# A second layer norm that reads the raw row sums, and a new order of a planned transformer block on one core

## The chip, the core and the metric

The kernel runs on one core of a Trainium2 chip. Its engines work side by side, each through its own list of instructions in order: TensorE (PE) multiplies matrices, VectorE (DVE) and ScalarE (ACT) do element-wise work, GpSimd (POOL) and SyncE (SP) here mostly issue transfers (DMA). They wait for each other through semaphores. PE writes its results into PSUM, eight banks of 128 x 512 float32; everything else lies in SBUF, 128 partitions wide. The metric is the device time of one execution in microseconds (us), as the median of several runs.

## The reference

A pre-norm block on `x` of shape (1, 2048, 512) in bfloat16: local dilated attention, then a gated feed-forward part, each behind a layer norm and with a residual addition.

```python
def _layernorm(x, axis=-1, eps=1e-5):
    m = jnp.mean(x, axis=axis, keepdims=True)
    v = jnp.var(x, axis=axis, keepdims=True)
    return (x - m) / jnp.sqrt(v + eps)

# attention: 32 heads of 16, each row attends to itself and 7 earlier rows, 2 apart
logits = einsum("bhsd,bhswd->bhsw", q, kg) * 16 ** -0.5     # masked where the row is before 0
o = einsum("bhsw,bhswd->bhsd", softmax(logits), vg) @ wo

# feed-forward, F = 1376
gate = einsum("bsd,df->bsf", x, W_gate); up = einsum("bsd,df->bsf", x, W_up)
y = einsum("bsf,fd->bsd", where(gate > 0, gate, 0) * up, W_down)

h  = x + attention(_layernorm(x))
h2 = h + feed_forward(_layernorm(h))
```

## The kernel before

**Tiling.** The 2048 rows go in four chunks of 512 rows (`tk` 0 to 3), each made of four blocks of 128 rows (`j`). For every chunk the kernel normalizes the rows, transposes them, computes Q, K and V in transposed form (`qkv`, twelve groups of four matmuls, line 587), multiplies Q with eight shifted K on DVE (`pr`, lines 638 and 653), sums over each head on PE (`sc`, lines 644 and 689), takes exponentials on ACT (`ex`), adds and inverts the denominators (`es`, `den`, `dl`, `dr`), scales the weights (`am`, line 747), spreads them over the partitions of each head by broadcast transfers on SP (`bd`, line 763, four for each half of the window), multiplies with eight shifted V (`mu`, lines 795 and 810), and sums the eight products (`tree`): the first halving by an accumulating transfer issued by POOL (`ta`, line 838), the others on DVE (lines 798 and 832). The output projection (`wo`, line 876) follows, one group for each block of rows.

**The second norm.** `rs` (line 887) adds the projection to `x` in place and writes the row's sum to `sm`. `hnm` (line 452) multiplies this sum by -1/512 and stores the negative mean. Two steps read that: `hsq` on ACT (line 458) squares the centred row and accumulates the squares, and `hxn` on DVE (line 512) writes the centred row in bfloat16. The centred row is not divided by the standard deviation. Since the feed-forward part is a product of two linear terms, the missing factor is the reciprocal variance, and it is multiplied in at the end: `hrl` and `hre` (lines 479 and 486) form it from the accumulated squares by a logarithm and an exponential, and `o` (lines 1006 and 1008) scales the down projection with it and adds the residual. Centred rows are transposed either on PE (`htp`, line 546, with a copy from PSUM, `hte`, line 562) or by a transposing transfer on SP (`htd`, line 535), which is the way of chunks 1 to 3.

**The feed-forward part.** The gate and up matmuls (`mm0` to `mm4`, line 949) take the transposed rows; ACT copies the up part (`ue`, line 953) and applies the rectifier to the gate part (`ge`, line 956), DVE multiplies them (`gu`, line 977). The last 96 of the 1376 columns are computed with rows on the partitions (`mm5`, line 916; `ge5`, `gu5`, lines 922 and 926) and transposed on SP (`gtd`, line 935). The down projection (`dn`, line 1000) reads eleven such tiles, the first eight in one step and the last three in another. In the last chunk the last block of rows is cut into columns 0 to 256, 256 to 384 and 384 to 512 (`dn3`, `dn4`, `dn5`). Results are stored by SP (`os`, line 1014), that of `dn5` by the ACT queue; those of chunks 0 and 1 go through an accumulating transfer (`oa`, line 1029) and a store (line 1032).

**Setup and head.** The first loads stand in a fixed order in `setup()`: row blocks of `x` on SP and ACT, three of the four chunks of the Q and K weights on the ACT queue (line 324) and the fourth on SP (line 339), behind a small POOL memset (line 338) that delays it. In chunk 0 the first six groups of Q and K are cut into pieces: `a` and `d` (row blocks 0 and 1, first two weight chunks), `b` (both blocks, last two weight chunks), `c` and `e` (row blocks 2 and 3). One `a` or `d` piece is two matmuls of 128 columns.

**What sets the order.** The work is not emitted where it is written. `add` collects 760 steps, each with its engine, an assumed duration and what it waits for, and gives it the number at its place in the list `RANK` as its priority. `order` then takes the steps strictly by rank. On each engine the steps therefore run in the order of their ranks, whatever the assumed durations are. The durations, the due times of loads (`XT`, `WT`) and the model of transfers (`dq`) decide only which of several equal buffers a step gets: the one that by the plan comes free first.

Of the kernel before, what the change touches and what calls it, by code (L numbers as in the profile page):

```python
# [93 lines left out]
class Plan:  # L94
# [21 lines left out]
    def order(self):  # L116
# [4 lines left out]
        while left:  # L121
# [80 lines left out]
def kernel(  # L202
# [23 lines left out]
    PRE = ((3,0),(3,1))  # L226
    PRD = ()
# [8 lines left out]
    CS = 512  # L236
# [21 lines left out]
    eps_t = sb.tile([P, 1], F32, name="eps_t")  # L258
# [57 lines left out]
    def setup():  # L316
# [11 lines left out]
        nc.gpsimd.memset(eps_t[:], EPS)  # L328
# [49 lines left out]
    XT = (3.1, 3.25, 4.1, 5.9, 7.15, 8.65, 9.0, 9.4, 12.9, 14.85)  # L378
    WT = (8.35, 8.35, 7.0, 11.5, 16.15, 25.5, 19.6, 29.0)
# [16 lines left out]
    TTM, DTG, ATE = 0.0845, 0.35, 0.3  # L396
# [5 lines left out]
    MM, TP = 0.2165, 0.057  # L402
    SW = 0.21
    PEL = 0.22
    A5, A10, AX, AS = 0.485, 0.91, 0.75, 0.21
    AL = 0.13
    D2, D5, D10, D20, D40, DST, DSM = 0.33, 0.61, 0.60, 1.14, 2.2, 0.61, 0.09
# [29 lines left out]
    def layernorm(tk, src, dst_slots, pr, groups, on_act, residual=None):  # L437
# [7 lines left out]
        for grp in groups:  # L445
            ag, nms = [], {}
            gk = str(grp[0]) if len(groups) > 1 else ""
            lo, hi = grp[0], grp[-1] + 1
            for j in grp:
                if residual:  # L450
                    def f_nm(j=j):
                        V.tensor_scalar(out=mv.t[:, j, 0:1], in0=sm.t[:, j:j + 1], scalar1=-1.0 / D,  # L452
                                        scalar2=None, op0=ALU.mult)

                    h = src[j][1] if tk in RPE else None

                    def f_sq(j=j, h=h):
                        nc.scalar.activation(out=junk[:, j % 2, :], in_=h.t[:] if h else x_sm[:, tk * BPC + j, :],  # L458
                                             func=ACT.Square,
                                             bias=mv.t[:, j, 0:1], scale=1.0, accum_out=sq.t[:, j:j + 1])  # L460

                    a = nms[j] = add((ln + "nm" + gk, tk), "DVE", DSM, f_nm, [src[j][0]], pr, take=[mv], use=[sm], lat=DL)
                    ag.append(add((ln + "sq" + gk, tk), "ACT", 0.66 if h else 0.72, f_sq, [a], pr,
                                  take=[sq], use=[mv] + ([h] if h else []), lat=AL))
# [625 lines left out]
```

## Time and profile before

| what | value |
|---|---|
| median of three timed runs | 192.83 us (192.31 to 192.97) |
| the profiled execution, its own time | 193.22 us |
| its span, first to last instruction | 191.3 us |
| granted PE clock, mean | 0.997 of full speed |
| busy: PE, DVE, ACT, POOL | 185.3, 149.6, 115.2, 18.5 us |
| moved by DMA | 26.44 MB |

The profile comes from one execution. Busy times are sums of instruction durations on one engine, overlaps counted once; ends of matmuls are modelled, so a busy PE need not be at its peak. PEld is the loading of stationary weights, which overlaps with PE's matmuls. A line such as L512 is line 512 of the kernel. "x16 | 5.1, 348" after a group means sixteen instructions, 5.1 us busy in all, 348 ns each on the mean. A q behind an engine's name (SPq, ACTq) means its sequencer, which issues transfers and waits.

### The profile page before, as it was taken

To read this page: it belongs to the slowest core of one execution; us is meant where nothing else is said; L and a number is where in the kernel's file an instruction comes from. 1 tells how busy PE (TensorE), PEld (TensorE's weight loads), DVE (VectorE), ACT (ScalarE), POOL (GpSimd) and SP (SyncE) were. 2 spreads that over 40 slices of the span, in tenths; PEclk is the share of its full clock that TensorE was granted. 3 is DMA by queue.
4 is the path that set the end of the run, shared out by engine and by line. 5 is a ranking of instruction groups with operands and counts; after the bars stand their busy time and mean duration, and the time that the engine had idled before them with its cause. 6 is when DMAs were issued, how large, how long until landed. Compare 5 with 4: busy or idle time off the path is not lost.

```text
span 191.3 us, 3033 instructions
## 1 busy us (share of the span) xinstructions
PE 185.3 (97%) x1101; PEld 96.5 (50%) x1120; DVE 149.6 (78%) x246; ACT 115.2 (60%) x236; POOL 18.5 (10%) x34
## 2 busy tenths in 40 slices
PE   7899999999999999999999999999999999999993
PEld 7795555544455444644445544444446444445452
DVE  6899999999999999999999987999627503212632
ACT  2589999976748967753454875144855528517500
POOL 3000002500000042000055000042100000000000
PEclk9999999999999999999999999999999999999998
DMA  5998464992068589993479916779900460120302
GB/s 159 331 351 327 102 157 84 200 196 45 0 258 228 168 154 193 183 279 61 88 131 186 203 33 139 164 151 186 211 4 0 82 165 0 31 82 0 82 25 88
DMA packets 26718, 26.44 MB, mean 138 GB/s; under 512 B 12528, under 2 KB 22608, under 8 KB 26704
## 3 DMA queue, kind: packets, MB, share of 16 engines
q1 hardware_dynamic: 23248, 16.39, 30.9%
q0 software_dynamic: 2736, 8.91, 25.1%
q10 hardware_dynamic: 720, 0.95, 1.5%
q8 instruction: 9, 0.15, 0.3%
q14 instruction: 5, 0.04, 0.1%
HBM read 8.42 MB, written 2.10 MB: 55 GB/s over the span
## 4 chain that ended last, share of the span: by engine, by line
PE 94%; DMA 3%; issue 1%; ACTq 0%; DVE 0%
PE bank L949 36%; PE bank L587 22%; PE bank L1000 20%; PE bank L876 7%; DMA wqk_sb<-in_A_wqkv_dram 3%; PE bank L644 3%; PE bank L916 3%; PE bank L546 2%; PE bank L689 1%; PE bank L720 0%; ACTq L324 0%; ACTq L322 0%; DVE row L1008 0%
## 5 line engine op out<-in xcount | busy, mean ns | idle before, releaser
L949 PE MATMUL bank<-quad,wgu_sb 128*128 128x512 bf16 x311 | 72.1, 379 | 0.4
L949 PEld LDWEIGHTS <-wgu_sb 128*128 128x128 bf16 x320 | 30.9, 98 | 36.9 <-issue 1.7
L1000 PE MATMUL bank<-wd_sb,gT 128*128 128x512 bf16 (+3 forms) x195 | 39.6, 355 | 0.2
L956 ACT ACTIVATE gr<-bank 128x512 bf16<-128x512 f32 x40 | 23.2, 607 | 17.0 <-PE bank L949 13.0
L977 DVE TENSOR_TENSOR gT<-gr,up_sb 128x1024 bf16<-128x1024 bf16 x20 | 13.7, 688 | 23.5 <-ACT up_sb L953 20.3
L587 PE MATMUL bank<-quad,wqk_sb 128*128 128x512 bf16 (+2 forms) x171 | 30.0, 319 | 1.0 <-DMA wqk_sb<-in_A_wqkv_dram 0.7
L953 ACT CAST up_sb<-bank 128x512 bf16<-128x512 f32 x40 | 22.6, 594 | 10.5 <-PE bank L949 8.5
L1000 PEld LDWEIGHTS <-gT 128*128 128x128 bf16 (+1 forms) x198 | 18.5, 98 | 19.9
L638 DVE TENSOR_TENSOR big<-quad,kT 128x4096 bf16<-128x4096 bf16 x11 | 24.9, 2283 | 0.0
L587 PEld LDWEIGHTS <-wqk_sb 128*128 128x128 bf16 x176 | 16.9, 114 | 11.2 <-DMA wqk_sb<-in_A_wqkv_dram 0.9
L795 DVE TENSOR_TENSOR big<-big,vT 128x4096 bf16<-128x4096 bf16 x9 | 20.2, 2282 | 0.0
L458 ACT ACTIVATE junk<-x_sm,mv 128x512 bf16<-128x512 bf16 x16 | 11.7, 730 | 10.0 <-DVE mv L452 9.9
L587 PE MATMUL bank<-quad,wv_sb 128*128 128x512 bf16 x63 | 15.6, 379 | 0.1
L876 PE MATMUL bank<-wo_sb,quad 128*128 128x512 bf16 x63 | 15.2, 379 | 0.1
L838 POOL DMA_DIRECT2D big<-big x12 | 11.2, 1018 | 38.5 <-PE bank L587 29.4
L887 DVE SCALAR_TENSOR_TENSOR x_sm<-x_sm,bank 128x512 bf16<-128x512 bf16 x16 | 10.5, 680 | 3.7 <-PE bank L876 3.7
L798 DVE TENSOR_TENSOR big<-big 128x1024 bf16<-128x1024 bf16 (+2 forms) x18 | 11.5, 655 | 0.1
L1008 DVE SCALAR_TENSOR_TENSOR row<-bank,iv,x_sm 128x512 bf16<-128x512 f32 (+2 forms) x10 | 6.2, 640 | 6.8 <-PE bank L1000 6.8
L469 DVE BATCH_NORM_STATS2 st<-x_sm 128x6 f32<-128x512 bf16 x16 | 10.3, 681 | 1.2 <-DMA x_sm<-in_A_x_dram 1.2
L595 ACT CAST kT<-bank 128x512 bf16<-128x512 f32 x16 | 9.1, 592 | 2.8 <-DVE big L638 2.8
L595 ACT CAST quad<-bank 128x512 bf16<-128x512 f32 x16 | 9.4, 596 | 2.1 <-PE bank L587 1.9
L595 ACT CAST vT<-bank 128x512 bf16<-128x512 f32 x16 | 9.4, 596 | 2.0 <-PE bank L587 2.0
(79 smaller groups left out, 173.7 us busy)
## 6 DMA issues: line engine op xcount, KB each, us to landing
big<-big POOLq DMA_DIRECT2D x12, 512.0 KB, 5.7
big<-ex SPq DMA_DIRECT2D x32, 128.0 KB, 2.7
wqk_sb<-wqk_sb POOLq DMA_DIRECT2D x3, 512.0 KB, 4.5
wgu_sb<-in_B_W_gate_dram SPq DMA_DIRECT2D x1, 1376.0 KB, 11.2
wgu_sb<-in_B_W_up_dram SPq DMA_DIRECT2D x2, 688.0 KB, 4.7
wd_sb<-in_B_W_down_dram SPq DMA_DIRECT2D x2, 640.0 KB, 5.2
x_sm<-in_A_x_dram SPq DMA_DIRECT2D x2, 512.0 KB, 7.2
x_sm<-up_sb POOLq DMA_DIRECT2D x4, 256.0 KB, 5.1
```

The costliest lines, as they stand in the source:

```text
L458: nc.scalar.activation(out=junk[:, j % 2, :], in_=h.t[:] if h else x_sm[:, tk * BPC + j, :], func=ACT.Square, bias=mv.t[:, j, 0:1], scale= ...
L587: nc.tensor.matmul(mm.t[:, lo:hi], lhsT=wv_sb[:, dt, t:D:NT] if c == 2 else wqk_sb[:, dt, c * D + t:(c + 1) * D:NT], rhs=xnT.t[:, dt, lo:h ...
L595: nc.scalar.copy(out=o, in_=mm.t[:])
L638: V.tensor_tensor(out=pb.t[:].rearrange("p (t w) s -> p t w s", t=2), in0=q4, in1=k4, op=ALU.mult)
L795: V.tensor_tensor(out=mt.t[:], in0=ab.t[:], in1=v8, op=ALU.mult)
L798: V.tensor_tensor(out=mt.t[:, 0:n, :], in0=mt.t[:, 0:n, :], in1=mt.t[:, n:2 * n, :], op=ALU.add)
L876: nc.tensor.matmul(od.t[:], lhsT=OT.t[:, t, j * P:(j + 1) * P], rhs=wo_sb[:, t, :], start=(t == 0), stop=(t == NT - 1 and tk not in RPE))
L949: nc.tensor.matmul(mm.t[:fs, lo:hi], lhsT=wgu_sb[:, dt, g, ft * P: ft * P + fs], rhs=hnT.t[:, dt, lo:hi], start=(dt == 0), stop=(dt == NT ...
L953: nc.scalar.copy(out=ub.t[:fs, i, :], in_=um.t[:fs, :])
L956: nc.scalar.activation(out=gr.t[:fs, i, :], in_=gm.t[:fs, :], func=ACT.Relu)
L977: V.tensor_tensor(out=gt.t[:fs, 0:n, :], in0=gr.t[:fs, 0:n, :], in1=ub.t[:fs, 0:n, :], op=ALU.mult)
L1000: nc.tensor.matmul(od.t[:, c0:c1], lhsT=gts[ft].t[:fs, ft % 2, j * P:(j + 1) * P], rhs=wd_sb[:fs, ft, c0:c1], start=(ft == 0), stop=(ft == ...
```

## The change

The sixteen `hnm` steps are gone. The square on ACT and the centring on DVE read the raw sum `sm` that `rs` wrote: the centred row is now 512 x minus the sum, 512 times its former value, and the accumulated square is 512 squared times the former one. To fit, the logarithm takes an epsilon that is 512 squared times as large, from a second column of `eps_t`, and a second small memset on POOL fills it. The reciprocal variance comes out smaller by the same 512 squared, so the result of the block is the same.

All ranks are new (744 steps). The planner's assumed durations, due times and transfer model are changed too, and so is a branch `PRE2` for one more halving before the scores, which is switched off (`PRE2 = ()`). Three differences in the order are named later. In the head, the `b` piece of group 1 on PE comes after seven instead of nine `a` and `d` pieces. On SP, around the second norm of chunk 1 and the broadcasts of chunk 2: `bd1S.2, ldd.1, bd0S.2, htd.1, gtd.0, htd.1, htd.1, htd.1` has become `ldd.1, gtd.0, bd0S.2, bd1S.2, htd.1 x4` (`.2` is the chunk; `ldd.1`, part of the down weights, stands directly behind `ldd.0` now). At the end, PE finishes with `dn3, dn5` instead of `dn5, dn4`.

```diff
 RANK = [
-    1, 2, 3, 4, 5, 6, 7, 8, 9, 10, 18, 11, 12, 13, 14, 15, 16, 17, 0, 19,
...
+    0, 1, 2, 3, 4, 5, 6, 7, 8, 9, 18, 10, 11, 13, 14, 15, 16, 17, 12, 19,
...
-                    late = 3.0 if at < free.get("DT", -1.0) + 0.8 else 0.0
+                    late = 3.0 if at < free.get("DT", -1.0) - 0.5 else 0.0
...
-    eps_t = sb.tile([P, 1], F32, name="eps_t")
+    eps_t = sb.tile([P, 2], F32, name="eps_t")
...
-        nc.gpsimd.memset(eps_t[:], EPS)
+        nc.gpsimd.memset(eps_t[:, 0:1], EPS)
+        nc.gpsimd.memset(eps_t[:, 1:2], EPS * D * D)
...
-    XT = (3.1, 3.25, 4.1, 5.9, 7.15, 8.65, 9.0, 9.4, 12.9, 14.85)
-    WT = (8.35, 8.35, 7.0, 11.5, 16.15, 25.5, 19.6, 29.0)
+    XT = (3.45, 3.65, 4.05, 5.3, 7.15, 8.65, 9.0, 9.4, 13.0, 14.5)
+    WT = (8.35, 8.35, 7.0, 10.85, 15.8, 25.5, 19.2, 29.0)
...
-    MM, TP = 0.2165, 0.057
+    MM, TP = 0.2158, 0.056
...
-                    def f_nm(j=j):
-                        V.tensor_scalar(out=mv.t[:, j, 0:1], in0=sm.t[:, j:j + 1], scalar1=-1.0 / D,
-                                        scalar2=None, op0=ALU.mult)
...
-                                             bias=mv.t[:, j, 0:1], scale=1.0, accum_out=sq.t[:, j:j + 1])
-
-                    a = nms[j] = add((ln + "nm" + gk, tk), "DVE", DSM, f_nm, [src[j][0]], pr, take=[mv], use=[sm], lat=DL)
+                                             bias=sm.t[:, j:j + 1], scale=-float(D), accum_out=sq.t[:, j:j + 1])
...
                     nc.scalar.activation(out=rs.t[:, lo:hi], in_=sq.t[:, lo:hi], func=ACT.Ln,
-                                         bias=eps_t[:, 0:1], scale=1.0 / D)
+                                         bias=eps_t[:, 1:2], scale=1.0 / D)
...
-                    V.tensor_scalar(out=xn.t[:], in0=x, scalar1=mv.t[:, j, 0:1], scalar2=None, op0=ALU.add)
+                    V.tensor_scalar(out=xn.t[:], in0=x, scalar1=float(D), scalar2=sm.t[:, j:j + 1], op0=ALU.mult, op1=ALU.subtract)
...
-                ms = [m] = [add(("ta%d" % t, tk), "POOL", 1.0, f_da, ms, tpr, use=[mt], lat=1.1, dq=(0.75, 2.74))]
+                ms = [m] = [add(("ta%d" % t, tk), "POOL", 1.0, f_da, ms, tpr, use=[mt], lat=1.1, dq=(-0.1, 2.78))]
```

More of the change, by code (lines that the diff above doesn't have):

```diff
@@ L226 @@
     PRE = ((3,0),(3,1))
+    PRE2 = ()
     PRD = ()
@@ L445, in layernorm @@
         for grp in groups:
-            ag, nms = [], {}
+            ag = []
             gk = str(grp[0]) if len(groups) > 1 else ""
@@ L459, in f_sq @@
                                              func=ACT.Square,
-                                             bias=mv.t[:, j, 0:1], scale=1.0, accum_out=sq.t[:, j:j + 1])
-                    a = nms[j] = add((ln + "nm" + gk, tk), "DVE", DSM, f_nm, [src[j][0]], pr, take=[mv], use=[sm], lat=DL)
-                    ag.append(add((ln + "sq" + gk, tk), "ACT", 0.66 if h else 0.72, f_sq, [a], pr,
-                                  take=[sq], use=[mv] + ([h] if h else []), lat=AL))
+                                             bias=sm.t[:, j:j + 1], scale=-float(D), accum_out=sq.t[:, j:j + 1])
+                    ag.append(add((ln + "sq" + gk, tk), "ACT", 0.66 if h else 0.72, f_sq, [src[j][0]], pr,
+                                  take=[sq], use=[sm] + ([h] if h else []), lat=AL))
                 else:
@@ L479, in f_ln @@
                     nc.scalar.activation(out=rs.t[:, lo:hi], in_=sq.t[:, lo:hi], func=ACT.Ln,
-                                         bias=eps_t[:, 0:1], scale=1.0 / D)
+                                         bias=eps_t[:, 1:2], scale=1.0 / D)
                 else:
                     nc.scalar.activation(out=rs.t[:, lo:hi], in_=mv.t[:, lo:hi, 1], func=ACT.Ln,
-                                         bias=eps_t[:, 0:1], scale=1.0 / D if sq else 1.0)
+                                         bias=eps_t[:, 0:1], scale=1.0)
             def f_ex(lo=lo, hi=hi):
@@ L509, in f_xn @@
                 if residual and on_act:
-                    nc.scalar.activation(out=xn.t[:], in_=x, func=ACT.Identity, bias=mv.t[:, j, 0:1], scale=1.0)
+                    nc.scalar.activation(out=xn.t[:], in_=x, func=ACT.Identity, bias=sn.t[:, j:j + 1], scale=float(D))
                 elif residual:
-                    V.tensor_scalar(out=xn.t[:], in0=x, scalar1=mv.t[:, j, 0:1], scalar2=None, op0=ALU.add)
+                    V.tensor_scalar(out=xn.t[:], in0=x, scalar1=float(D), scalar2=sm.t[:, j:j + 1], op0=ALU.mult, op1=ALU.subtract)
                 elif on_act:
@@ L522, in norm @@
                 f = lambda: f_xn(j, xn)
-                d, u = ([nms[j]], [mv]) if residual else ([e], [nb, rs] if on_act else [mv, rs])
+                d, u = ([src[j][0]], [sm]) if residual else ([e], [nb, rs] if on_act else [mv, rs])
                 if on_act:
                     return xn, add((ln + "xn" + gk, tk), "ACT", AX, f, d, pr, take=[xn], use=u, lat=AL)
-                return xn, add((ln + "xn" + gk, tk), "DVE", DXN, f, d, pr, take=[xn], use=u, lat=DL)
+                return xn, add((ln + "xn" + gk, tk), "DVE", 0.27 if residual else DXN, f, d, pr, take=[xn], use=u, lat=DL)
             step = 1 if tk == 0 and not residual else 2
@@ L684, with f_pb, f_sc @@
                 a = add(("pa%d" % hf, tk), "DVE", D40, f_pa, [a for a, _, _ in prd], apr, use=[b for _, b, _ in prd], lat=DL)
-                def f_sc(sc=sc, pb=prd[0][1]):
-                    for u in range(2):
+                nu = 2
+                if (tk, hf) in PRE2:
+                    def f_pb(p0=prd[0][1]):
+                        V.tensor_tensor(out=p0.t[:, 0:4, :], in0=p0.t[:, 0:4, :], in1=p0.t[:, 4:8, :], op=ALU.add)
+                    a = add(("pb%d" % hf, tk), "DVE", D20, f_pb, [a], apr, use=[prd[0][1]], lat=DL)
+                    nu = 1
+                def f_sc(sc=sc, pb=prd[0][1], nu=nu):
+                    for u in range(nu):
                         for g in range(4):
@@ L740 @@
             b = add(("den", tk), "PE", 2 * MM, f_dn, exd, apr + 2, take=[dn], use=exs, lat=PEL)
-        b = add(("dl", tk), "ACT", A5, f_ld, [b], apr + 2, use=[dn], lat=AL)
+        b = add(("dl", tk), "ACT", 0.56, f_ld, [b], apr + 2, use=[dn], lat=AL)
         rcd = add(("dr", tk), "ACT", A5, f_rc, [b], apr + 2, take=[rc], use=[dn], lat=AL)
@@ L861 @@
                     wload[n].append(add(("ld" + n, i), "SP", 0.45 + 0.1 * (n == "d" and i), lambda n=n, i=i: f_load(n, i),
-                                        [lg], 0, lat=1.0, dq=(1.0, 1.74)))
+                                        [lg], 0, lat=1.0 + 1.0 * (n == "d" and i), dq=(1.0, 1.74)))
         if tk == 1 and "d" in LATE:
@@ L894 @@
             else:
-                a = add(("rs%d" % j, tk), "DVE", 0.63, f_rs, [a], base + 50, take=[sm], use=[od], lat=DL)
+                a = add(("rs%d" % j, tk), "DVE", 0.613, f_rs, [a], base + 50, take=[sm], use=[od], lat=DL)
             hd.append((a, od))
```

18 lines of the change are left out of this document (9 added, 9 removed), and 74 rows, old and new, of the table RANK.

## The prediction, written before the changed kernel was run

> **What bounds the kernel now.** I read the page first, then the waits of TensorE (PE), the busy times by stretch, and the chain of work that ended last, in order of time.
>
> ```profile
> span 191.3 us, 3033 instructions
> ...
> PE 185.3 (97%) x1101; PEld 96.5 (50%) x1120; DVE 149.6 (78%) x246; ACT 115.2 (60%) x236; POOL 18.5 (10%) x34
> ...
> PE 94%; DMA 3%; issue 1%; ACTq 0%; DVE 0%
> ...
> PE bank L425 <- DVE warm L326: 1.0, 1, 1.0
> PE bank L587 <- DMA wqk_sb<-in_A_wqkv_dram: 0.7, 1, 0.7
> ```
>
> The first row says that PE is busy 97% of the span; since ends of matmuls are modelled, that alone proves little. The last two rows are all the waits of PE that the trace lists: one on the memset before the warm-up, and one on a load of weights. Behind that load PE never waits.
>
> ```profile
> 8.14:188.20 180.06, 178.97 (x1038) 90.71 (x1057) 143.25 (x222) 111.61 (x227) 16.65 (x19) 1.00 0.58 136
> 11.95:103.00 91.05, 90.42 (x542) 45.32 (x552) 90.77 (x127) 66.19 (x128) 11.59 (x14) 1.00 0.69 164
> 188.20:191.30 3.10, 0.00 (x0) 0.00 (x0) 0.35 (x1) 0.00 (x0) 0.00 (x0) 0.83 0.23 64
> ```
>
> Columns: length, then busy time of PE, weight loads, DVE, ACT, POOL, the granted clock, the DMA share. From 8.14 to 188.20 PE is busy 178.97 of 180.06 us at a clock of 1.00. In the second row, up to 103, DVE is full as well (90.77 of 91.05 us).
>
> ```profile
> 1.67 6.42 DMA wqk_sb<-in_A_wqkv_dram
> 8.09 0.05 issue
> 8.14 0.81 PE bank L587 x11
> 8.95 0.22 PE bank L546 x4
> 9.17 0.22 PE bank L587 x4
> ...
> 175.14 3.45 PE bank L949 x16
> ...
> 188.20 0.35 DVE row L1008
> ```
>
> So the time has three parts: a head of 8.14 us that ends when the second of four loads of Q and K weights lands (8.09), 180.06 us of PE work end to end, and a tail of 3.10 us. A 512-wide matmul takes 3.45 / 16 = 0.216 us, a 128-wide one 0.22 / 4 = 0.055 us. The diff removes, adds and resizes no matmul, so the middle cannot shrink by more than the 1.1 us that separates 178.97 from 180.06, and it grows by every wait that the new order brings.
>
> The profiled execution took 193.22 us, 1.92 us beyond its span. The median of the three timed runs is 192.83, their range 192.31 to 192.97; they spread by 0.34%, so I take 0.3% (0.58 us) as what a measurement can tell from no change. The sum is made against 193.22 and then carried to the median, 0.39 lower.
>
> **The removed scaled sums.** Sixteen small DVE instructions go, four in each chunk of 512 rows.
>
> ```profile
> L458 ACT ACTIVATE junk<-x_sm,mv 128x512 bf16<-128x512 bf16 x16 | 11.7, 730 | 10.0 <-DVE mv L452 9.9
> ...
> L512 DVE TENSOR_SCALAR row<-x_sm,mv 128x512 bf16<-128x512 bf16 x16 | 5.1, 348 | 0.3
> ...
> L452 DVE TENSOR_SCALAR mv<-sm 128x1 f32<-128x1 f32 x16 | 2.1, 146 | 0.1
> ...
> L517 DVE TENSOR_SCALAR row<-x_sm,mv,rs 128x512 bf16<-128x512 bf16 x4 | 1.5, 402 | 0.0
> ...
> L328 POOL MEMSET eps_t<- 128x1 f32 x1 | 0.1, 98 | 0.0
> ```
>
> Columns of a group: count, then total busy time in us and mean ns of one, then idle time before it and who ended it. L452 is what goes: at most 16 x 0.146 = 2.3 us of DVE. The centring L512 becomes a multiplication by 512 and a subtraction. Its price is not in the trace; one operation with one per-row scalar takes 348 ns (L512), two with two scalars 402 ns (L517). I take 375 ns, the middle: 16 x 0.027 = 0.4 us is given back (bounds 0 and 0.9). The square L458 keeps its form with another scale and bias: 730 ns as before. It waited 9.9 us in all for L452; ACT is idle there, and nothing but the reciprocal variance for the last addition needs it. Net, DVE saves 1.4 to 2.3 us, and each centring can start some 0.15 us sooner. None of that shortens the run by itself: PE, which reads the results, waited for DVE nowhere behind 8.14. It widens margins only, and PE's own work is the cover that remains. The second memset of the epsilons delays the rest of POOL's setup by at most 0.1 us (L328, 98 ns); it is hidden, since PE's first work hangs on the load in the chain above, which the ACT queue issues.
>
> **The new order, head.** I numbered the steps as the code adds them, dropped the sixteen, and read each engine's sequence from both lists of ranks. Up to the first piece that needs the third and fourth weight chunks (the b piece of group 1), PE had 8.5 two-matmul pieces and two groups of transposes behind 8.14; now it has 6.5 and two. It gets there 2 x 2 x 0.055 = 0.22 us sooner.
>
> ```profile
> 3.74 0.33 SPq L339 DMA_DIRECT2D wqk_sb<-in_A_wqkv_dram  x1
> ...
> DMA to landing us min/median/max: 5.7/5.7/5.7
> ...
> 9.46 6.30 PE L587 MATMUL bank<-quad,wqk_sb 128*128 128x128 bf16 x63
> ```
>
> The fourth chunk (L339) lands at 3.74 + 5.7 = 9.44. The x63 row starts with the last early piece (0.11 us); the b piece's first matmul is at 9.57 and its second, 256 wide, at 9.68, the first to need the fourth chunk: 0.24 us after landing. Moved up by 0.22 it stands at 9.46, and with the 0.05 us that the chain shows between landing and matmul it waits 0.03 to 0.06 us. I take 0.05; the ends are 0 (an earlier landing) and 0.22 (a later one, when the old order's extra pieces would still have covered it). The next place where PE depends on DVE, the scores of chunk 0, gets nothing: ahead of the second half's scores PE has the same matmuls as before, and DVE the same eight products.
>
> **The new order, tail.** The last PE piece was the third quarter of the last row block (dn4), stored by SP; now it is the fourth (dn5), stored by the ACT queue.
>
> ```profile
> out_dram<-row SPq DMA_DIRECT2D x1, 64.0 KB, 2.3
> out_dram<-row ACTq DMA_DIRECT2D x1, 32.0 KB, 1.6
> out_dram<-row SPq DMA_DIRECT2D x1, 32.0 KB, 1.4
> ```
>
> Same size, 1.6 instead of 1.4 us from issue to landing: +0.2 us. The half block before it (64 KB, 2.3 us) is ready some 0.55 us earlier, 11 matmuls of a quarter, so it lands within 0.4 us of the last: the upper end is +0.6, and the lower 0. I take 0.2, the row of the same size and queue.
> The Trainium skill ("DMA: Bandwidth & Descriptors", section "Issuing engines are not separate DMA queues") says that the issuing engine only changes the time of issue. By that rule the tail would cost nothing and the sum would be 0.2 us lower.
>
> **The new order, middle.** Hand-offs from DVE to PE get wider: the output projection of chunk 1 now has eight more matmuls ahead of it (8 x 0.216 = 1.7 us, part of chunk 0's down projection), and so has that of chunk 2. The tightest that depends on transfers is chunk 1's second norm.
>
> ```profile
> 80.01 0.41 DVE L747 TENSOR_TENSOR ex<-ex,rec 128x512 bf16<-128x512 bf16 x1
> ...
> 81.45 2.51 SPq L763 DMA_DIRECT2D big<-ex  x4
> ...
> 89.18 0.62 DVE L512 TENSOR_SCALAR row<-x_sm,mv 128x512 bf16<-128x512 bf16 x2
> ...
> 90.41 3.87 SPq L535 DMA_TRANSPOSE quad<-row  x3
> ...
> 95.86 1.47 PE L949 MATMUL bank<-quad,wgu_sb 128*128 128x512 bf16 x6
> ```
>
> The landings of L535 (transposes) and of L763 (broadcasts), least, median and most:
>
> ```profile
> DMA to landing us min/median/max: 2.4/2.5/3.0
> ```
>
> ```profile
> DMA to landing us min/median/max: 2.5/2.7/5.4
> ```
>
> Before, the last of four transposes was issued at 90.41 + 2 x 1.29 = 92.99 and landed 2.5 us on, at 95.5: 0.4 us ahead of the gate and up matmuls at 95.86. Now both groups of four broadcasts for chunk 2 stand directly ahead of the four transposes on SP. The group that waits for the scaling at 80.01 (L747) now comes first, and the other, scaled earlier, queues behind it. DVE has six more steps ahead of that scaling.
>
> ```profile
> L977 DVE TENSOR_TENSOR gT<-gr,up_sb 128x1024 bf16<-128x1024 bf16 x20 | 13.7, 688 | 23.5 <-ACT up_sb L953 20.3 <-ACT gr L956 2.3 <-PE bank L1000 0.9
> ...
> L798 DVE TENSOR_TENSOR big<-big 128x1024 bf16<-128x1024 bf16 x13 | 8.7, 683 | 0.0
> ...
> L832 DVE TENSOR_TENSOR quad<-big 128x512 bf16<-128x512 bf16 x9 | 3.6, 419 | 0.1
> L926 DVE TENSOR_TENSOR row<-gr,bank 128x192 bf16<-128x192 bf16 x8 | 2.7, 348 | 0.5 <-ACT gr L922 0.5
> ```
>
> One L977, one wide addition (L798), two L926 and two of the 512-wide additions (L832) make 0.69 + 0.68 + 2 x 0.35 + 2 x 0.42 = 2.9 us; four L452 of chunk 0, at most 0.6, are gone. So the scaling ends near 80.01 + 0.41 + 2.9 - 0.6 = 82.7, and SP is busy with eight broadcasts until 82.7 + 2 x 2.51 = 87.7. The fourth transpose goes out at 87.7 + 3 x 1.29 = 91.6 and lands at 94.1, some 1.8 us ahead. The centred rows are in time: the last was ready at 89.18 + 0.62 = 89.80, and is needed at 91.6. So I put 0 on the middle.
>
> Sum: 0.05 + 0.2 + 0 = +0.25 us, 193.22 to 193.47, or 193.1 on the median.
>
> **Rivals.**
> Slower, by the SP queue at chunk 1. Eight broadcasts go out without a pause just ahead of the transposes; before, the first four had gone out ahead of the down-weight load. If the transposes land as late as the slowest broadcast did (5.4 us), the last comes at 91.6 + 5.4 = 97.0 and PE waits 1.1 us: 193.1 + 1.1 = 194.2. It decides from a landing of 4.3 us on (91.6 + 4.3 = 95.9). For it: the broadcast row's maximum. Against it: the transposes' own maximum of 3.0, and that the down-weight load that stood among those broadcasts on SP now goes out a chunk earlier.
> Faster. The timed runs may hold waits that the profiled one does not show, for before's margin here is only 0.4 us, and the wider margins remove them. The price is bounded by the best run: 192.83 becomes 192.3, or 192.2 if the head and tail costs fail to show. Against it: the one execution seen without any wait was also the longest of the four, so the spread looks like the landing that ends the head, which stays.
> No difference: both terms vanish, 192.8.
>
> **How the numbers follow.** Forecast 0.42 (192.6 to 193.4), no difference 0.13, the SP queue 0.23, a wait of over 0.5 us at a hand-off that I did not name 0.11 (some 193.8), faster 0.11. So faster 0.11, within 0.3% 0.55, slower 0.34. The range reaches to both rivals, the slower one with half of the tail's upper end on top: 192.2 to 194.4.
>
> **What would show it.** In the changed profile: no L452 group; the centring group near 375 ns; again a single PE wait on the weights, with a second of about 0.05 us at L587 near 9.5; PE busy some 179 us behind it; the last transfer issued by the ACT queue, and a tail near 3.3 us. A row of PE or its weight loads that waits for a transposed tile near 96 us, or for DVE, would prove me wrong on the slow side, a head well under 8.1 us or a tail under 3.0 on the fast side.

## The result and the profile after

The changed kernel takes 193.54 us (median of 12 runs, 192.59 to 194.28); the kernel before, measured beside it, 192.87 (12 runs, 192.18 to 193.34). The ratio is 1.0038, with a 95% interval of 1.0022 to 1.0053: slower by 0.4 to 1.0 us, 0.7 in the middle. The forecast was 193.1, within 192.2 to 194.4. The profiled execution took 194.09 us, with a span of 192.3.

The page of the changed kernel: its span, the busy times, the shares of the chain, and two groups (columns as in the prediction).

```profile
span 192.3 us, 3058 instructions
...
PE 186.7 (97%) x1120; PEld 96.4 (50%) x1120; DVE 149.2 (78%) x230; ACT 114.7 (60%) x236; POOL 18.5 (10%) x35
...
PE 76%; DVE 9%; DMA 6%; ACT 5%; issue 1%; SPq 1%; DVEq 0%
...
L456 ACT ACTIVATE junk<-x_sm,sm 128x512 bf16<-128x512 bf16 x16 | 11.6, 725 | 8.6 <-DVE x_sm L891 8.6
...
L509 DVE TENSOR_SCALAR row<-x_sm,sm 128x512 bf16<-128x512 bf16 x16 | 5.3, 351 | 0.2
```

The sixteen small instructions are gone, the centring (L509) costs 351 ns instead of 348, and the square (L456) 725 instead of 730. But PE now has 76% of the chain that ended last; it had 94%. The waits of PE in the changed kernel:

```profile
PE bank L584 <- ACT kT L592: 1.0, 1, 1.0
PE bank L427 <- DVE warm L327: 1.0, 1, 1.0
PE bank L953 <- DMA quad<-row: 0.4, 1, 0.4
PE bank L584 <- DMA wqk_sb<-in_A_wqkv_dram: 0.3, 1, 0.3
```

Two waits are new: one before a QKV group (L584), which the trace puts down to a copy on ACT, and one before the gate and up products (L953), for a transposing transfer. The busy times by stretch of the changed kernel:

```profile
7.80:189.53 181.73, 180.32 (x1057) 90.62 (x1057) 143.42 (x208) 111.65 (x228) 16.61 (x19) 1.00 0.57 133
...
32.42:33.69 1.27, 0.28 (x2) 0.00 (x0) 1.27 (x2) 1.27 (x4) 1.27 (x2) 1.00 0.04 7
...
96.55:97.18 0.63, 0.30 (x2) 0.00 (x0) 0.63 (x1) 0.63 (x2) 0.00 (x0) 1.00 0.04 3
...
189.56:192.31 2.75, 0.00 (x0) 0.00 (x0) 0.34 (x1) 0.00 (x0) 0.00 (x0) 1.00 0.35 107
```

The head is 7.80 us (before 8.14), the PE stretch 181.73 (before 180.06), the tail 2.75 (before 3.10). So the loss sits in the middle, where the forecast had put nothing, and the tail has become shorter, not longer. In the second and third row PE issues no weight load for the whole stretch: these are the two waits.

**The first wait, near 33 us.** Weight loads of PE in the changed kernel and in the kernel before, in order of time (start, length, in brackets the idle time before):

```profile
30.59 1.62 PEld L584 LDWEIGHTS <-wv_sb 128*128 128x128 bf16 x8
33.69 1.23 PEld L584 LDWEIGHTS <-wqk_sb 128*128 128x128 bf16 x7 [1.47 <-issue]
```

```profile
31.79 0.60 PEld L587 LDWEIGHTS <-wqk_sb 128*128 128x128 bf16 x4
32.49 0.42 PEld L546 LDWEIGHTS <-row 128*128 128x128 bf16 x4
33.11 1.44 PEld L587 LDWEIGHTS <-wqk_sb 128*128 128x128 bf16 x8 [0.20 <-issue]
```

The load at 33.69 belongs to the first QKV group of chunk 3 (step `qkv4.3`), which reads the four blocks transposed by SP (`xtd.3`). The issue of the last of these transfers, in the changed kernel and in the one before:

```profile
30.51 1.22 SPq L532 DMA_TRANSPOSE quad<-row  x1
```

```profile
30.49 1.27 SPq L535 DMA_TRANSPOSE quad<-row  x1
```

Its time from issue to landing, in the same order:

```profile
DMA to landing us min/median/max: 3.1/3.1/3.1
```

```profile
DMA to landing us min/median/max: 2.5/2.5/2.5
```

To two decimals it landed at 33.59, and the weight load started 0.10 us later; before, it landed at 33.01 and the load started at 33.11. In the instruction list this load waits for the four transfers alone. The matmul behind it does wait for ACT, to have its bank, but that bank's copy was over by 30.3; the copy that the trace names (ended 33.65) is of another bank. Before, PE waited for this landing too, but briefly. Two groups of transposes of chunk 2 (L546, 0.44 us) stand ahead of it, the second of them directly, and behind that one the weight loads stood idle for 0.20 us (the bracket in the row of 33.11). The matmuls of PE there:

```profile
32.70 0.39 PE L546 MATMUL bank<-identity,row 128*128 128x128 bf16 x4
33.15 1.89 PE L587 MATMUL bank<-quad,wqk_sb 128*128 128x512 bf16 x8
```

The four transposes start at 32.70 and follow each other by 0.055 us, so PE was free for the next matmul at 32.92 and waited 0.2 us. No list of waits has this, since the modelled end of the last transpose (33.09) leaves a gap of only 0.06 us.

In the new order ACT copies Q and K of chunk 1 first and normalizes chunk 2 later, so that these transposes stand behind `qkv4.3` and only the sum of the denominators (0.2 us) has come ahead of it; and the transfer itself took 0.6 us longer (what comes together with that stands in the last section). The weight load ahead of this place ended at 32.22 (33.69 less the 1.47 in brackets), against 32.91 before, also because PE's head had ended 0.34 us sooner in this execution. By the starts of its matmuls PE waits 1.2 us here.

**The second wait, near 97 us.** SP around the second norm of chunk 1, and the weight loads of PE, both of the changed kernel:

```profile
82.84 1.23 SPq L939 DMA_TRANSPOSE gT<-row  x1
84.50 5.89 SPq L767 DMA_DIRECT2D wqk_sb<-ex  x8
90.48 5.39 SPq L532 DMA_TRANSPOSE quad<-row  x4
```

```profile
95.37 0.98 PEld L1004 LDWEIGHTS <-gT 128*128 128x128 bf16 x6 [0.42 <-issue]
97.18 0.78 PEld L953 LDWEIGHTS <-wgu_sb 128*128 128x128 bf16 x5 [0.83 <-issue]
```

This is the place that the slow rival named. The fourth transpose was issued at 94.45, not 91.6, and landed at 97.08, not 94.1.

### The profile page after: what moved, and what is told of

Its sections match the earlier page's. It is cut to its first block, busy times and chain, and to the rows that moved or that the text cites. A ratio compares the mean times of both kernels' runs of the same rounds, so it can differ in the third digit from the quotient of the medians.

```text
span 192.3 us, 3058 instructions
## 1 busy us (share of the span) xinstructions
PE 186.7 (97%) x1120; PEld 96.4 (50%) x1120; DVE 149.2 (78%) x230; ACT 114.7 (60%) x236; POOL 18.5 (10%) x35
## 4 chain that ended last, share of the span: by engine, by line
PE 76%; DVE 9%; DMA 6%; ACT 5%; issue 1%; SPq 1%; DVEq 0%
PE bank L953 36%; PE bank L1004 16%; PE bank L584 11%; PE bank L880 7%; DVE big L650 4%; DVE st L466 3%; PE bank L920 3%; DMA x_sm<-in_A_x_dram 3%; ACT row L511 2%; PE bank L641 2%; DMA wqk_sb<-ex 1%; DMA quad<-row 1%; ACT kT L592 1%; PE bank L543 1%; DVE big L635 1%
## 5 line engine op out<-in xcount | busy, mean ns | idle before, releaser
L953 PE MATMUL bank<-quad,wgu_sb 128*128 128x512 bf16 x320 | 72.0, 379 | 0.4 <-DMA quad<-row 0.4
L953 PEld LDWEIGHTS <-wgu_sb 128*128 128x128 bf16 x320 | 31.0, 98 | 37.1 <-issue 1.7
L1004 PE MATMUL bank<-wd_sb,gT 128*128 128x512 bf16 (+3 forms) x198 | 40.2, 355 | 0.0
L584 PE MATMUL bank<-quad,wqk_sb 128*128 128x512 bf16 (+2 forms) x176 | 30.4, 321 | 1.3 <-ACT kT L592 1.0
L584 PEld LDWEIGHTS <-wqk_sb 128*128 128x128 bf16 x176 | 16.9, 113 | 12.4 <-issue 1.9
L842 POOL DMA_DIRECT2D big<-big x13 | 11.7, 963 | 61.8 <-DVE big L799 30.5
L456 ACT ACTIVATE junk<-x_sm,sm 128x512 bf16<-128x512 bf16 x16 | 11.6, 725 | 8.6 <-DVE x_sm L891 8.6
L584 PE MATMUL bank<-quad,wv_sb 128*128 128x512 bf16 x64 | 16.3, 380 | 0.0
L799 DVE TENSOR_TENSOR big<-big,vT 128x4096 bf16<-128x4096 bf16 x6 | 13.5, 2286 | 0.0
L802 DVE TENSOR_TENSOR big<-big 128x1024 bf16<-128x1024 bf16 (+2 forms) x19 | 12.2, 658 | 0.1
L1010 ACT ACTIVATE up_sb<-bank,iv 128x512 bf16<-128x512 f32 x8 | 5.1, 691 | 11.3 <-PE bank L1004 11.3
```

The source lines that it names most:

```text
L584: nc.tensor.matmul(mm.t[:, lo:hi], lhsT=wv_sb[:, dt, t:D:NT] if c == 2 else wqk_sb[:, dt, c * D + t:(c + 1) * D:NT], rhs=xnT.t[:, dt, lo:h ...
L799: V.tensor_tensor(out=mt.t[:], in0=ab.t[:], in1=v8, op=ALU.mult)
L802: V.tensor_tensor(out=mt.t[:, 0:n, :], in0=mt.t[:, 0:n, :], in1=mt.t[:, n:2 * n, :], op=ALU.add)
L953: nc.tensor.matmul(mm.t[:fs, lo:hi], lhsT=wgu_sb[:, dt, g, ft * P: ft * P + fs], rhs=hnT.t[:, dt, lo:hi], start=(dt == 0), stop=(dt == NT ...
L1004: nc.tensor.matmul(od.t[:, c0:c1], lhsT=gts[ft].t[:fs, ft % 2, j * P:(j + 1) * P], rhs=wd_sb[:fs, ft, c0:c1], start=(ft == 0), stop=(ft == ...
```

## The experiments

For each run I read four moments from one profiled execution: when the last chunk-3 block landed and the load that needs it started; when PE began its first step behind the first 220 steps (up to there, some 39 us, both orders have the same 220 steps, so they can be combined); how long PE took from there to its last matmul; and the tail behind that.

| kernel | time, us | ratio to before (95%) | landed, load | step 221 | to last matmul | tail |
|---|---|---|---|---|---|---|
| before | 192.87 | | 33.01, 33.11 | 39.64 | 148.57 | 3.10 |
| changed | 193.54 | 1.0038 (1.0022 to 1.0053) | 33.59, 33.69 | 40.45 | 149.11 | 2.75 |
| arith_only | 192.81 | 0.9991 (0.9970 to 1.0011) | 32.31, 32.42 | 38.94 | 148.56 | 3.08 |
| order_only | 194.15 | 1.0059 (1.0038 to 1.0080) | 33.24, 33.34 | 40.09 | 149.03 | 2.76 |
| early_old | 192.87 | 0.9995 (0.9975 to 1.0015) | 33.48, 33.58 | 40.11 | 148.58 | 2.75 |
| late_old | 193.51 | 1.0024 (1.0001 to 1.0047) | 33.19, 33.29 | 40.05 | 148.56 | 3.13 |
| sp_swap | 193.18 | 1.0018 (0.9990 to 1.0047) | 33.06, 33.16 | 39.92 | 149.57 | 2.75 |
| fill_sp | 192.63 | 0.9990 (0.9965 to 1.0016) | 33.13, 33.23 | 39.54 | 149.28 | 2.77 |
| early_old_sp | 192.55 | 0.9991 (0.9969 to 1.0013) | 32.74, 32.84 | 39.37 | 149.00 | 2.75 |
| sp_early | 193.61 | 1.0029 (1.0004 to 1.0054) | 33.63, 33.74 | 40.49 | 148.78 | 3.11 |
| fill_sp_early | 193.09 | 1.0002 (0.9983 to 1.0021) | 33.03, 33.13 | 39.44 | 148.98 | 3.12 |
| pool_pad | 192.24 | 0.9967 (0.9943 to 0.9992) | 33.11, 33.22 | 39.74 | 148.56 | 2.81 |
| before_pad | 192.32 | 0.9974 (0.9954 to 0.9994) | 32.90, 33.00 | 39.53 | 148.57 | 2.74 |
| pad4 | 193.03 | 1.0005 (0.9974 to 1.0036) | 32.84, 32.95 | 39.47 | 148.57 | 3.15 |

The kernel before was measured again beside each set of runs (medians 192.81 to 193.04); the ratios are against those.

**Arithmetic or order.** `arith_only` is the kernel before with the arithmetic of the change and its old ranks; `order_only` is the changed kernel with the old arithmetic put back.

```diff
 arith_only, against the kernel before
-V.tensor_scalar(out=mv.t[:, j, 0:1], in0=sm.t[:, j:j + 1], scalar1=-1.0 / D, ...)
-V.tensor_scalar(out=xn.t[:], in0=x, scalar1=mv.t[:, j, 0:1], scalar2=None, op0=ALU.add)
+V.tensor_scalar(out=xn.t[:], in0=x, scalar1=float(D), scalar2=sm.t[:, j:j + 1], op0=ALU.mult, op1=ALU.subtract)
...
 order_only, against the changed kernel: the reverse, each hnm behind its rs
```

> The old order, with the sixteen scaled sums left out and the centring changed: the arithmetic of the change alone. Theory A (the time lost comes from the order alone): DVE gets about 1.5 us emptier, PE was waiting for it nowhere, so within 0.2 us of the kernel before, 192.7 to 193.1, and PE shows only the waits on the warm-up memset and on the Q and K weights. Rival B (the dearer two-operation centring delays the transposes of the second norm): 0.3 to 0.7 us slower than before, with a PE wait behind a transposed tile.

> The new order with the old arithmetic, each scaled sum put directly behind the residual addition that feeds it. Theory A (order alone): as slow as the changed kernel or slightly slower, 0.5 to 0.9 us above before, with a PE wait of about 1 us near 33 us. Rival B (the arithmetic): within 0.2 us of before.

The arithmetic alone shows no change (0.9991, 1 within the interval), the order alone loses 0.6%, which is some 1.1 us and more than the 0.5 to 0.9 expected. DVE's busy time fell from 149.6 to 148.0 us in the old order and from 151.4 to 149.2 in the new one: 1.6 and 2.2 us saved. In the old order no time is gained by it; whether it gains some 0.2% in the new one (1.0038 with it, 1.0059 without) the overlapping intervals leave open. PE's wait near 33 us is there in `order_only` (1.0 us). Theory A stands: the loss comes from the order.

**Which part of the order.** One kernel has the old order for the first 220 steps and the new one behind, the other the reverse.

```diff
 early_old
-first 220 steps by the new ranks
+first 220 steps by the old ranks
 late_old
-steps 221 to 744 by the new ranks
+steps 221 to 744 by the old ranks
```

> The changed kernel, but with its first 220 steps (up to about 39 us; both orders have the same 220 steps there) in the old order; all later steps in the new one. Theory A1 (the loss is the wait for the last chunk-3 transpose near 33 us): that wait of 1.0 to 1.25 us shrinks below 0.3 us, DVE is no longer late, the transposes of chunk 1 land in time near 95.5 us, and the time is 192.4 to 193.0, at or below the kernel before. Rival A2 (the loss is in the later order, the SP queue at chunk 1): PE arrives near 96 us earlier, so its wait there grows from 0.4 to about 1.2 us, and the time stays at 193.4 to 193.8.

> The reverse: the changed kernel with its first 220 steps in the new order and all later ones in the old order. Theory A1 (the loss is the wait near 33 us): the wait of 1.0 to 1.25 us is there, and the time is 0.6 to 1.2 us above before, 193.5 to 194.1. Rival A2 (the later order): within 0.2 us of before, 192.7 to 193.1.

With the old start the loss is gone (0.9995), with the new start it is there (1.0024, with an interval that only just excludes 1). The weight loads of PE at the start of chunk 3, in `early_old` and then in `late_old`:

```profile
32.66 0.42 PEld L543 LDWEIGHTS <-row 128*128 128x128 bf16 x4
33.58 1.44 PEld L584 LDWEIGHTS <-wqk_sb 128*128 128x128 bf16 x8 [0.50 <-issue]
```

```profile
33.29 1.44 PEld L584 LDWEIGHTS <-wqk_sb 128*128 128x128 bf16 x8 [1.32 <-issue]
```

In all fourteen profiles of the table this load starts 0.10 or 0.11 us behind the last landing. The seven kernels with the old start begin step 221 at 38.94 to 40.11, 39.54 on the mean; the five with the new start (without the move below) at 39.92 to 40.49, 40.20 on the mean: 0.66 us is lost up to there. Of these, 0.43 are the landing (33.34 on the mean, against 32.91; the last transfer is issued no later, at 30.34 against 30.45, but takes 3.00 us against 2.46), and 0.23 the PE work that now stands behind it. Behind step 221 PE takes 148.56 to 148.58 us in the seven kernels that have neither the second wait nor a move on SP, and 149.03 and 149.11 in the two that have the wait and no such move. With the old start the second wait vanishes too, but only just: the last block landed at 96.11, its load started at 96.21, and PE got there at the same moment. The expectation for `early_old` had 95.5 there, and for its time 193.0 at most; 192.87 agrees, though the 0.35 us of its shorter tail do not show in it (the interval has room for them). Its first wait did not shrink below 0.3 us as expected: PE waited 0.5 us for a landing that came late, at 33.48.

**The second wait.** The four broadcasts of chunk 2 that are ready early (`bd1S.2`) were put ahead of the four that are ready late.

```diff
-ldd.1 gtd.0 bd0S.2 bd1S.2 htd.1 x4
+ldd.1 gtd.0 bd1S.2 bd0S.2 htd.1 x4
```

> The changed kernel with one move on SP: the four broadcasts of chunk 2 whose scaled weights are ready early go ahead of the four that wait for the late scaling near 84 us. Theory A (the second wait, 0.4 to 0.5 us near 97 us, comes from eight broadcasts behind the late scaling): only four are left behind it, the last transpose of chunk 1 lands 2 us or more earlier, the stretch of PE behind step 220 falls from 149.1 to 148.6 us, and the time by about 0.5 us to 192.9 to 193.2; the wait near 33 us stays. Rival B: the landing near 97 us hangs on the transposes themselves, the wait stays, 193.4 to 193.7.

A miss: the wait stayed. SP in `sp_swap`:

```profile
82.46 1.23 SPq L939 DMA_TRANSPOSE gT<-row  x1
83.81 6.38 SPq L767 DMA_DIRECT2D wqk_sb<-ex  x8
90.29 5.17 SPq L532 DMA_TRANSPOSE quad<-row  x4
```

The early four could not start early, since `gtd.0` (L939) ahead of them on SP waits for DVE until 82.46; all eight still go out in a row, in 6.4 us. The time of 193.18 tells this kernel apart neither from the changed one nor from the one before. So the move was made larger:

```diff
-ldd.1 gtd.0 bd0S.2 bd1S.2 htd.1 x4
+ldd.1 bd1S.2 gtd.0 bd0S.2 htd.1 x4
```

> The changed kernel with one move on SP: the four early broadcasts of chunk 2 go ahead of the transposing transfer of the gated part (issued at 82.84 us in the changed kernel), not only ahead of the four late ones. The smaller move left all eight behind 83.8 us, because that transfer waits for DVE until then, and the landing near 97 us stayed. Theory A (the second wait comes from eight broadcasts issued in a row behind the late scaling): the early four are issued from about 79.8 us, only four are left behind the scaling at 84.4, the last transpose of chunk 1 is issued near 92.4 and lands near 95 us, the second wait is gone, and PE's stretch behind step 220 falls from 149.1 to 148.6 us; 192.9 to 193.2. Rival B: the transposes land as late as before for a reason of their own, and the second wait of 0.4 to 0.6 us stays.

SP in `sp_early`, and then its weight loads:

```profile
79.74 2.50 SPq L767 DMA_DIRECT2D big<-ex  x4
82.87 1.23 SPq L939 DMA_TRANSPOSE gT<-row  x1
84.48 3.83 SPq L767 DMA_DIRECT2D big<-ex  x4
88.41 5.15 SPq L532 DMA_TRANSPOSE quad<-row  x4
```

```profile
96.51 1.40 PEld L953 LDWEIGHTS <-wgu_sb 128*128 128x128 bf16 x7
```

The last transpose landed at 94.76 and the wait is gone, as theory A said: the stretch behind step 221 is 148.78 us instead of 149.11. The time, 193.61, is above the 192.9 to 193.2 expected: a wait of 0.2 us at 129 us has come instead, and the tail of this kernel is 3.11 us again, which takes back what the wait gave. Why is shown under the tail.

With the old start and the smaller move:

> The changed kernel with its first 220 steps in the old order and the move on SP. With the old start the last transpose of chunk 1 landed 0.10 us ahead of its first use in the one profile seen, so some executions may have waited. Theory A: with 2 us of slack there nothing of either wait is left, the tail is 2.75 us, and the time is 0.2 to 0.4 us below before, 192.4 to 192.6. Rival B (no execution waited there): the same as without the move, 192.8 to 192.9.

The transposes landed at 95.34, 0.14 us ahead of their load, so there was little slack, not 2 us. At 192.55 the expected time came out, but the interval takes in no gain at all as well, and the stretch behind step 221 got 0.42 us longer, 0.33 of it through a wait at 128 us, before chunk 2's gate products. All five kernels with a move on SP have such a wait at 128 to 130 us, of 0.18 to 0.33 us between the starts of matmuls; I did not follow its cause.

**The first wait, by filling it.** Two normalizations of chunk 2 on ACT (and the DVE step ahead of them) go up by a few steps, so that two groups of PE transposes stand ahead of `qkv4.3`.

```diff
 PE
-qkv10.1 qkv4.3 qkv0.3 xtp.2 qkv1.3 xtp.2 ...
+qkv10.1 xtp.2 xtp.2 qkv4.3 qkv0.3 qkv1.3 ...
 ACT
-qe5.1 qe11.1 qe6.1 dl.0 xxn.2 xxn.2 qe7.1 ...
+qe5.1 qe11.1 xxn.2 xxn.2 qe6.1 dl.0 qe7.1 ...
```

> As the previous one, and two normalizations of chunk 2 on ACT with the small DVE step ahead of them moved up by a few steps, so that two groups of PE transposes (0.44 us) go ahead of the first product of chunk 3 and not behind it. Theory A (PE waits there for the last transposed block of chunk 3, whose landing does not hang on PE or ACT): PE arrives 0.44 us later at the same landing, does 0.44 us less behind it, and the time falls by another 0.3 to 0.45 us against the previous kernel, to 192.5 to 192.8. Rival B (PE waits there for ACT's copy that frees a bank, as the profile lists it): ACT's copies are later, so PE's wait stays or grows, and nothing or less than nothing is gained.

> The same with the two transposes of chunk 2 also moved ahead of the first product of chunk 3. Theory A: both waits are nearly gone, and what remains of the new order's difference is its tail, 0.35 us shorter: 192.3 to 192.6. Rival B (the new order has further waits that these two hide): 192.7 to 193.1, with a PE wait of 0.2 us or more at a new place.

The weight loads of `fill_sp` at this place:

```profile
32.09 0.33 PEld L584 LDWEIGHTS <-wv_sb 128*128 128x128 bf16 x2
32.52 0.65 PEld L543 LDWEIGHTS <-row 128*128 128x128 bf16 x8
33.23 1.88 PEld L584 LDWEIGHTS <-wqk_sb 128*128 128x128 bf16 x10
```

The load at 33.23 follows the landing (33.13) as ever, but PE's matmuls now run without a gap up to it. The copy on ACT that the trace had named runs from 33.24 to 33.86 here, so it ends 0.6 us after the load that was said to wait for it: this settles it between the transfer and ACT. Both kernels begin step 221 at 39.44 to 39.54, as with the old start, and `fill_sp` takes 192.63 us, 0.55 less than `sp_swap`, in the expected range; the two intervals overlap, so it is the moments of the profile that carry this reading. Behind step 221 it still loses 0.7 us: 0.2 in the second wait, 0.2 in the wait at 129 us and 0.3 in a late start of chunk 1's scores at 42.7 us. `fill_sp_early` comes out at 193.09, at the upper end of rival B: its tail is 3.12, and 0.41 us more is spent behind step 221, in the wait at 128 us and a late start of chunk 1's scores at 42.6 us.

**The tail.** In the profiles of the first four experiments and of the two kernels the tail is 3.08 to 3.13 us with the old ending and 2.75 or 2.76 with the new one. The last store itself takes the same: 1.45 us by SP, 1.47 by ACT. The difference comes after it has landed (1.28 us to the end, or 0.90), in the closing sequence, which all fourteen kernels here run through. POOL's four closing instructions of one kind there, first and last start, in the kernel before and in the changed one:

```profile
L1085 POOLq EVENT_SEMAPHORE  x4: 17/17/17, 190.2 to 191.2; - x4
```

```profile
L1089 POOLq EVENT_SEMAPHORE  x4: 17/17/17, 191.6 to 192.2; - x4
```

They span 1.0 us in the one and 0.6 in the other. Counted through POOL's records, a pause of 0.39 to 0.43 us stood ahead of the 69th each time that it fell in the closing: as the last of 69 in the kernel before, as the last but one of 70 in `arith_only` and `late_old` (one more memset). The three with the new ending have 75 or 76 records, with five or six more semaphore instructions ahead of the closing, and there the 69th falls before or at POOL's long wait for the last store. So eight memsets that nothing reads were put at the end of POOL's list, where it has been idle since about 136 us.

```diff
         for op in todo:
             if op.fn is not None:
                 op.fn()
+        for _ in range(8):
+            nc.gpsimd.memset(pad[:], 0.0)
```

> The kernel with the new arithmetic in the old order, and eight memsets of a 128 x 1 tile that nobody reads, added as POOL's last steps (POOL is idle there from about 136 us on). In the profiles so far the closing sequence of POOL has a gap of 0.40 to 0.43 us directly ahead of its 69th recorded instruction, in all three kernels that end in the old order; in the three that end in the new order POOL has 5 or 6 instructions more, its 69th comes while it has nothing to do, and the tail behind the last matmul is 2.75 instead of 3.08 to 3.13 us. Theory C (the tail hangs on where POOL's 69th instruction falls): with eight more the gap leaves the closing sequence, the tail is 2.7 to 2.8 us and the time 0.3 to 0.4 us below that of the new arithmetic in the old order, 192.4 to 192.6. Rival D (the tail hangs on the last store's engine or on the order of the last stores): tail 3.08 to 3.13 us, 192.7 to 192.9.

> The kernel before, unchanged but for nine memsets of a 128 x 1 tile that nobody reads, as POOL's last steps. Theory C (the gap of 0.4 us ahead of POOL's 69th instruction stands in the closing sequence): tail 2.7 to 2.8 us instead of 3.10, time 0.3 to 0.4 us below before, 192.4 to 192.6. Rival D (it was the new arithmetic in the padded kernel that gained): within 0.15 us of before.

> As the padded kernel with the new arithmetic in the old order, with four added memsets in place of eight: POOL then records 74 instructions and its 69th is the sixth from the end, inside the closing sequence and behind the wait for the last store. Theory C (a gap of 0.4 us ahead of POOL's 69th instruction, wherever that falls): the gap stands inside the closing sequence again, five instructions ahead of the last, the tail is 3.08 to 3.13 us and the time 192.7 to 192.9. Rival E (any POOL work late in the run keeps POOL awake and shortens the closing): tail 2.75 to 2.8 us, 192.2 to 192.5.

`pool_pad` and, without any of the change, `before_pad` (nine memsets, likewise 78 records): the span of the four instructions is 0.6 us in both, the tail 2.81 and 2.74 us, and the times 192.24 and 192.32. Each is below both kernels, 0.33% and 0.26% under the one before, with intervals that exclude no gain; the expectations had 192.4 to 192.6. With four memsets the 69th stands inside the closing again, and so does the pause. The same row of `pool_pad` and of `pad4`:

```profile
L1084 POOLq EVENT_SEMAPHORE  x4: 17/17/17, 190.4 to 191.0; - x4
```

```profile
L1084 POOLq EVENT_SEMAPHORE  x4: 17/17/17, 190.0 to 191.1; - x4
```

Tail 3.15 us, time 193.03: for the closing sequence theory C holds, and by the tail, 3.15 against 2.81, it is excluded that some late POOL work as such would do it (the intervals of the two times still touch). Outside the closing no pause shows: in `pool_pad` and `before_pad` the 69th is one of the added memsets, and it starts 0.06 us behind the end of the one ahead. The count explains `sp_early` and `fill_sp_early` too: their other choice of buffers left POOL 70 records, and the pause was back.

## Why the prediction was right and wrong

The time fell inside the range, 0.44 us above the point, and just past the bound of what a measurement can tell: it is the slower case, which had 0.34. That the range held is in part luck: it reached past 193.4 for a rival with another mechanism, and the tail, forecast as a loss, gave back 0.35 us of what the middle lost. The larger part of the loss came at a hand-off that the prediction did not name: it had a chance of 0.11 for such a wait, at some 193.8, and no working. By profiles the change is +0.66 up to step 221, +0.50 behind it (149.07 on the mean of two, against 148.57), and -0.35 in the tail: +0.8, against 0.7 (0.4 to 1.0) measured.

- **The removed sums: right.** DVE saves 1.6 us in the old order (estimate 1.4 to 2.3), and that gains nothing. The centring costs 351 ns where 375 was taken; the lower bound was right. One thing was not foreseen: the new order has DVE busy for 1.2 us (148.0 to 149.2) longer with the same instructions.
- **Head: +0.05, measured 0.** The `b` piece shows no wait; the fourth chunk had landed at 9.14 and the piece began at 9.13. This was the lower end.
- **Tail: +0.2, measured -0.35: wrong in sign.** The 1.6 us of the row stood for a single store; as the last store of the changed kernel it takes 1.47. By the Trainium skill ("DMA: Bandwidth & Descriptors", section "Issuing engines are not separate DMA queues") the tail should have cost nothing, and for the store itself the trace agrees: 1.47 and 1.45 us. What changed, the closing sequence, was in neither account: I had cut the tail at the landing.
- **Middle: 0, measured +1.2. This is the step that failed.** I took chunk 1's second norm as the tightest hand-off that depends on transfers and wrote that hand-offs get wider. The tightest was the landing of chunk 3's transposes, where there was no margin at all: in the trace of before PE already waited 0.2 us for it. "Behind that load PE never waits" was read from the list of waits, which leaves this one out. The new order put 0.23 us of PE work behind that landing, and the last block came 0.43 us later on the mean. Behind it, the second norm of chunk 1 cost another 0.5.
- **The SP rival: right place, wrong term.** It was priced at 1.1 us through slow landings; the last transposes landed in 2.4 to 3.1 us, as I had argued. The start was late: the fourth went out at 94.45, not 91.6. Of the 2.85 us, 1.7 come from the scaling (84.42 instead of 82.7: 0.8 from the late start, 0.4 because leaving out the four sums of chunk 0 freed 0.2 us of DVE time and not 0.6, the rest are idle moments of DVE ahead of it) and 0.9 from the eight broadcasts (5.9 us instead of 5.0; one of them took 1.38 us to issue). PE lost 0.5 us there, since it was late itself.

The forecast's test, a weight load of PE that waits for a transposed tile near 96 us, did show. The other such load, 63 us earlier, was the larger.

## What to carry to other kernels

Before a change of order is priced, list for each group of PE work that reads a transfer the margin between its landing and the moment at which PE is free for it, and do not rely on the list of waits: the place with the smallest margin, here none, is where the new order bites first, and work taken from ahead of it is paid in full. A wait of a matmul is best read at its weight load: if that one starts a fixed moment behind a landing, the transfer is the cause, whatever the list of waits names. And a tail has an end of its own behind the last landing, which may hang on things as remote as the number of instructions on an idle engine.

## What the runs showed of the hardware

- POOL's 69th recorded instruction is preceded by a pause of 0.39 to 0.43 us wherever it falls in the closing sequence (before, `arith_only`, `late_old`, `sp_early`, `fill_sp_early`, `pad4`), and costs nothing where POOL waits anyway; among the added memsets of `pool_pad` and `before_pad` there is no such pause. The Trainium skill ("Runtime: NRT & Kernel Launch", section "Instruction fetch mechanics") says that instructions are streamed in blocks of 256 and that crossing a block's end is mostly hidden. A pause bound to a count would fit a block's end; here 0.4 us of it was not hidden. In the pause itself the queues list no transfer of instructions. But in all six profiles one packet of 8 KB of the kind `instruction` on queue q14 starts 0.67 to 0.92 us behind the 69th. In four of the other eight it starts 0.36 to 1.26 us behind the 69th, at 135 to 137 us, and in the remaining four, where the 69th is the first instruction of the closing, 1.2 us behind the end of POOL's last long wait before it (a DRAIN), at 142 to 144 us. So the count goes with a fetch; that the pause is part of it is argued and not shown.
- The four transposing transfers of chunk 3 have the same shape, but one of them often takes 3.0 to 3.2 us and not 2.5: the third with the old start (in four of seven profiles; the fourth always took 2.44 to 2.52), the fourth with the new one (in four of seven; the third always took 2.45 to 2.48). In the new order, which issues the four blocks in another sequence, the slow one is the one for which PE waits. What goes with it stands in the DMA records: a packet of 8 KB of the kind `instruction` on queue q14 that starts while the transfer is under way. (In the changed kernel it starts at 32.32, in the one before at 30.37 us.) These transposes go out in groups of four, so the fourteen profiles have 168 second, third and fourth ones. In 20 of them such a packet starts 0.89 to 1.94 us behind the issue, and these took 2.58 to 3.41 us; of the other 148 one took 2.63 and the rest at most 2.52. At chunk 3 the packet starts at 29.6 to 30.7 us with the old start and at 31.3 to 33.1 with the new one, so it meets the third transfer in the one and, in six of seven profiles, the fourth in the other. That the packet is what delays the transfer was tested by no run.
- One of the eight broadcasts behind 84 us takes 0.9 to 1.9 us to issue where 0.6 is usual. In five of the six profiles with eight in a row that slow issue ended at 87.56 to 87.77 us, though it was the fourth, fifth or sixth of them; in `order_only` at 88.18. In all six a packet of 16 KB of the kind `instruction` on queue q8 starts at 85.9 to 86.4 us, and the slow issue ends 0.37 to 0.39 us behind the end of that packet. Here too no run tests which is the cause.
